# Scoring batch 0 head by head: one operation per head in place of one per query tile, with the order of operations searched anew

## The chip, the core and the metric

The kernel runs on one core of a Trainium2 chip. The metric is the device time of one launch in microseconds; smaller is better. Before the change three runs gave 567.77, 568.21 and 569.11 us, median 568.21 us. The core has a matrix engine (PE, TensorE), a vector engine (DVE), a scalar engine (ACT), a general engine (POOL, GpSimd) and a queue that issues transfers (SP). Each engine works through its own list of instructions in order.

## What is computed

Four batches of eight heads, 576 positions, head size 64. First attention with rotary positions, then a two-layer block with a parametric relu, then a soft mixture of eight experts with four slots each:

```python
q_rot, k_rot = rotate(q), rotate(k)
scores = scale * q_rot @ k_rot.T
attn = exp(scores - max(scores)); attn /= sum(attn) + 1e-09
x = attn @ v                              # 2304 x 512
h = x @ w_in                              # 512 -> 2048
x = (max(h, 0) + alpha * min(h, 0)) @ w_out
logits = x @ phi                          # 32 slots
# softmax over tokens gathers 32 slot inputs, 8 experts relu(s @ w1) @ w2,
# softmax over slots spreads the outputs back over 2304 rows
```

## The kernel before

The attention works on a pair of heads (four pairs per batch) and, in each pair, on four tiles of 128 query rows and a tail of 64. The two heads of a pair lie on the two halves of the 128 partitions: head 0 on partitions 0 to 63, head 1 on 64 to 127. For each tile and head PE computes 128 x 576 scores, as two pieces of 288 columns (j = 0, 1) that fill two banks of PSUM, the tile `st`. DVE takes the row maximum (`top`, L449), ACT the exponential and its sum (`expo`, L454) and adds a small constant (L471), DVE takes the reciprocal (L472), POOL scales the row (`norm`, L496).

In batch 0 PE then transposes the result (`turn`, L519, and `turn_c`, L570), ACT copies it out (L529, L574), and PE multiplies with v (L602). The later batches transpose on DVE and through a round trip to DRAM (`tb`, `sc`, `ET`), and their scores use two half-precise factors (`scores`, L444, one pass each), head by head.

In batch 0 the scores are plain 32-bit matmuls with a contraction of 64 (`plain`, L431). The operation `plain` scores both heads of a tile: for each j it issues head 0 and then head 1, each to its own `st` tile. It takes two `st` slots at once, and only two exist (`st=2` in the plan, 2 buffers of two banks in `ps_s`). So both slots have to be free before a tile is scored. The first tile of all is split by j instead: one operation for the left pieces of both heads, one for the right.

Next to batch 0 run the conversion of the first weight matrix into two half-precise parts (DVE L671 to L675, ACT L683 and L686, PE L248 and L249 `rest`, ACT L242 `dg` and L253), the folding of the second with phi (L724, L733), and the rotary products of the coming pairs on POOL (L331, L339). After batch 0 the first layer starts (L763 `ph`, twelve matmuls for a chunk).

Nothing in the program is scheduled while it runs. A table (`ORDER`) lists all operations of the plan in one order, `plan.order()` decodes it and checks that no operation stands before one that it needs and that no slot is taken before it is free, and the operations are then issued in that order, each to its engine.

Of the kernel before, what the change touches and what calls it, by code (L numbers as in the profile page):

```python
# [11 lines left out]
F32 = mybir.dt.float32  # L12
# [7 lines left out]
B, H, S, D = 4, 8, 576, 64  # L20
# [20 lines left out]
    "NvCW+tpA6dA6h1+XiTMD_B&Z5|7;rGKbW}ocQ+x7?zd^4_FK0jq^TI3Lv{lkl3DauRO_lYfup-m8We~}V?}1&%ko+tcc={cb6~e+)%dI}6AB|I1J71j|>D5(Ty(<wuwyg#0@>AQg-jpr"
    "p)Qw+T{y2Pt(^hEK1Ey~C;w*4$8dzQi;+In_T=KMR^0eT}_d&Nfc0le6*tz@{of+?Sg3We5-uU&-EqgYVs~VxzrNnLbp7JJ}vh%5_-"
    "z1u@U77vZMZP+l(%J}Nprg=HIDlt;L)+1ESOkZU=YgsFOB;*0gU6Srm#?l~s&yg4C4E$(d^n_0qr-"
    "}xQSlVhfAYmCkH}5Ys~)8fj67z1dy~~pt5%a+exl0pCU;>%a>~xTb0Was3_jXdwu3bAmYhtOP~)24Y*w}Ktl>A8hJVsIH|Ow%)1NnJG}G;JNBG0sqN;X`<;via$6q_Pe>51Qy-"
    ";i7?N5`ZXPdV<ms(}~BOd+eWe8cAV$yUj$9a`!V$w~&&AYM{^4t;5`|r+aUK;c61MJNlqWJd-$M^GcH^)+^Qtl{p{#*-JWo{=|M>DFm<k4mO8}G-(Z||r-"
    "cYYgW@BMLZP*$DQMenqd&G9=jn+znIuXH~>7Oq=D<xi8rx=U|!oSefVWdk25E?f#*>N{=U`b$?YP_X+zMTE<dBBkUaNoGgE`Lm;!ioT0^m_7<RWE0zD8+>3Y(|<<b^-"
    "%cA7@+w)mHI7pMU<jgV@sJTzMny{Cv@^((-"
    "kxI@7vG5u);s>PxjgayWr)uTbvB4%^;=RtaTDI0}K}pS#v0N7(8j7^=K@>S(pe<d<zHZCyn_0q5q!5lprQ)Y8_G53gfC*hZKgHoNyZX1a>d#oIzJxlv$9KTGDD*uw>e#^{uW}-"
    "7QSS>~OkX6g*!N@|mIvvwhna|B=<|adXmpx5ZM$UlEWPzK>+r9;HGL8W=|1IOgDc>xR>cIEI>))Ftu%A^IvUDKU}86-"
    "Blyj61bzjQ)VStEp19n~`>kp??cGD*bRcqd8#sn>JZ9#k9#_)cvvK{c(>7Xif<3H<g+Vp{=K-(wdvc;AV=y?&J`^JJ(9@EohM|8aBqwicy_i1tY-HcNKK`Sfq4HoAetc?T0nC?#Ph-"  # L50
    "H9bx=U3$6X$8!`Tc7LUu$`(>DBglC70ouhjgX2Gn{Nnbm9RQKx7N0cN4UY7BF_F4aBdOm|l=YQ$Ns6whYI;*~gHpBeytT)R&|esvnK#aDKEL?FJ8%xon{+=;$t*Lq`~|3n#peTt?tZt-"
    "J4b$es&~|OP()3TC&0Gt+kUnw-U{;Tsr%R1WmP!5mqzWX9J&$GV$Hh`d1r|3m5({bq=)<2NcZ{a?$LOmh&y(;g3{4}yeyr&RL3eZbS!-"
    "TLqgNVnGYjm8~YXLZTn%}(6@<y=2GL}@+wWqJ%HHjRcBU3Z<;lkEcro|62M-4HX``f=C48)MmHYtjf>seyp@vu9kj-0LgKXFoP$=A%ixg?IozP}6%`f~lr(N>-"
    "osRqo$U!P81Q}uUquFudgc7K!&AQ{HYn??@8ctv9h|9bz2>~+eHC7BDX01VH$cjaG4OsiBE>(~>CO0)BMo4AiS@1r#^Ui%;}5|vR}z&?!>Udj%^a%ik{7-"
    "Wcw}xVR!TFxy5YkRrL_GijGz0RPw3o9&BePVM;D!eE}iVbd0vm*60FBS%WGGF)v)ly0ymA!A>omZ0Q1kzl^>KrYZ!TzRmhsdueX@ASJ}k|w1Vv1Nk}rQ?iLTwOLOVaE`8;3cmChCtdFK"
    "g#lJJa)cR5=jNYYF*(y&M>zt>MhZN1*$WFS`6bctj$cd+boO`xKF9E>sPSEV(CU-AfACnfFJS}v-+m*oZX%^9uHN{q?DRATX#-nHM=$74(#lYrq<ufkpN-NC|&5HZa@il+dui3vw^yc;"
    "&h(478(ZKp!$aia>`tF;Qy<0R_Ms3hG{Hb~6P8p*Nyw!CElJr_`{<wqG0F}7Tx+x|l0my*X*K?g7$H<Q^nRPMbq|TXTQ7rYa{rZump$BeX7#J;s851G>^kG)p&-"
    "`#$$L$5BR`J(h%E3gF?g{3;OoUd+v+0+sNNq|Ma&*Zx#q_#Iw_~DLoqQhTdTB+{3?L(>xmJ552PFsUohl<O$4cEJTaFZ@y{3#e*%mw*P-"
# [1535 lines left out]
```

## Time and profile before

| | |
|---|---|
| time, median of three runs | 568.21 us |
| the profiled execution | 567.4 us, its span 565.5 us |
| PE busy | 534.2 us, 94% of the span |
| DVE, ACT, POOL busy | 453.1, 362.7 and 317.0 us |
| busy in the span by stretch | in the rows below |
| chain that ended last, by engine | PE 70%, POOL 8%, ACT 7%, DVE 7%, DMA 5% |

The span is the time from the first to the last instruction; the remaining 1.9 us lie around it. Busy times of PE include the tail of each matmul until its result is written, as the profile models it, so neighbouring matmuls overlap in them. A 32-bit matmul appears as two records, so the four matmuls of a tile of batch 0 appear as eight.

### The profile page before, as it was taken

Reading aid. Unit: us, or ns where it says so; the run is one execution under the profiler, and the core shown is the slowest. Engines: PE = TensorE matmul, PEld = TensorE weight load, DVE = VectorE, ACT = ScalarE, POOL = GpSimd, SP = SyncE. Lnnn points to the kernel's source line nnn. Section 1 sums busy time; section 2 is a strip of 40 time slices with the busy share of each in tenths; the row PEclk is TensorE's granted clock in tenths of the full one; section 3 lists DMA queues with packets and bytes.
Section 4 is the critical chain, followed back from the end, with each engine's and each line's share of the span. In section 5 each row is a group of like instructions: output and inputs, shape, how many; then the busy total and the mean of one; then the engine's idle time right before and its main releaser. Section 6 shows DMA issues by size and latency. Waiting matters only on the chain.

```text
span 565.5 us, 14971 instructions
## 1 busy us (share of the span) xinstructions
PE 534.2 (94%) x5770; PEld 395.0 (70%) x5770; DVE 453.1 (80%) x1049; ACT 362.7 (64%) x951; POOL 317.0 (56%) x299
## 2 busy tenths in 40 slices
PE   3789999999999999999999999999999999999984
PEld 1445545578877787787777688778778888863573
DVE  5699988898998788899898889898864899754541
ACT  2999989998878668878766778687342323330221
POOL 0799978889998668779884778675110000001000
PEclk9999999999999999999999999999999999999996
DMA  8963855435999987897999897879764999899988
GB/s 305 394 250 110 318 197 184 142 114 163 319 324 323 351 258 253 264 343 255 309 299 304 307 279 277 307 239 315 238 237 173 412 404 349 330 369 379 406 321 249
DMA packets 80807, 160.76 MB, mean 284 GB/s; under 512 B 5344, under 2 KB 44640, under 8 KB 80736
## 3 DMA queue, kind: packets, MB, share of 16 engines
q1 hardware_dynamic: 79408, 158.99, 80.5%
q8 instruction: 46, 0.75, 0.5%
q10 hardware_dynamic: 1328, 0.82, 0.5%
q14 instruction: 25, 0.20, 0.1%
HBM read 115.75 MB, written 36.96 MB: 270 GB/s over the span
## 4 chain that ended last, share of the span: by engine, by line
PE 70%; POOL 8%; ACT 7%; DVE 7%; DMA 5%; issue 2%; SPq 1%; ACTq 0%; POOLq 0%; DVEq 0%
PE ph L763 29%; PE pv L602 10%; PE st L444 8%; PE pu L955 3%; DMA sc<-tb 3%; POOL e L496 3%; PE lg L800 3%; PE ph L1286 3%; PE po L1345 2%; POOL xn L331 2%; PE pt L519 2%; DVE mm L449 2%; DMA vt<-in_v_dram 1%; PE pf L1470 1%; ACT e L454 1%
## 5 line engine op out<-in xcount | busy, mean ns | idle before, releaser
L763 PE MATMUL ph<-xt,w 128*128 128x256 f16 x1536 | 183.8, 273 | 0.0
L763 PEld LDWEIGHTS <-w 128*128 128x128 f16 x1728 | 162.1, 98 | 28.7 <-issue 6.2
L496 POOL TENSOR_SCALAR e<-e,mm 128x576 f32<-128x576 f32 x144 | 121.0, 849 | 72.5 <-DVE mm L472 60.7
L454 ACT ACTIVATE e<-st,mm 128x576 f32<-128x576 f32 x144 | 106.0, 736 | 31.5 <-DVE mm L449 25.1
L449 DVE TENSOR_REDUCE mm<-st 128x1 f32<-128x576 f32 x144 | 106.5, 743 | 16.9 <-PE st L444 10.3
L771 ACT ACTIVATE rl<-ph 128x256 f32<-128x256 f32 x144 | 53.3, 379 | 75.7 <-PE ph L763 66.6
L331 POOL TENSOR_TENSOR xn<-xn,tabs 128x576 f32<-128x576 f32 x60 | 91.5, 1538 | 4.5 <-DMA ks<-xn 2.2
L776 DVE SCALAR_TENSOR_TENSOR g<-rl,oma,ph 128x256 f32<-128x256 f32 x144 | 65.9, 465 | 22.4 <-ACT rl L771 21.8
L506 DVE STREAM_TRANSPOSE tb<-e 128x512 f32<-128x512 f32 (+1 forms) x108 | 75.3, 705 | 5.4 <-DMA sc<-tb 3.9
L602 PE MATMUL pv<-ET,vt 128*64 128x256 f32 (+1 forms) x640 | 77.0, 384 | 0.3 <-ACT ET L574 0.3
L444 PE MATMUL st<-ks,qs 128*128 128x288 f32 x384 | 73.9, 316 | 0.7 <-ACT e L454 0.6
L602 PEld LDWEIGHTS pv<-ET,vt 128*64 128x64 f32 (+1 forms) x640 | 42.4, 136 | 26.4 <-issue 5.2
L444 PEld LDWEIGHTS st<-ks,qs 128*128 128x128 f32 x384 | 54.4, 189 | 6.6 <-issue 2.5
L792 DVE STREAM_TRANSPOSE gb<-g 128x512 f32<-128x512 f32 x64 | 44.0, 694 | 0.1
L356 POOL TENSOR_TENSOR qs<-xn,qs 64x576 fp32r<-64x576 f32 x24 | 34.9, 1454 | 12.4 <-ACT qs L349 4.3
L471 ACT ACTIVATE mm<-mm,eps 128x1 f32<-128x1 f32 x144 | 39.6, 289 | 1.5
L431 PE MATMUL st<-ks 64*128 64x288 f32 (+1 forms) x168 | 30.2, 456 | 9.4 <-DVE ks L304 7.5
L975 POOL MEMSET edt<- 128x256 f32 x1 | 0.5, 497 | 66.6 <-DVE lp L944 66.6
L334 POOL TENSOR_TENSOR xn<-xn 128x576 f32<-128x576 f32 x24 | 34.8, 1454 | 0.9
L359 ACT ACTIVATE ks<-xn 64x576 fp32r<-64x576 f32 x48 | 32.7, 680 | 0.8
L431 PEld LDWEIGHTS st<-ks 64*128 64x128 f32 (+1 forms) x168 | 17.2, 191 | 19.0 <-DVE ks L304 8.4
L454 ACT ACTIVATION_READ_ACCUMULATOR e<-st,mm 128x1 f32 x144 | 28.3, 197 | 0.0
(171 smaller groups left out, 783.6 us busy)
## 6 DMA issues: line engine op xcount, KB each, us to landing
sc<-tb SPq DMA_DIRECT2D x48, 576.0 KB, 4.4
ET<-sc SPq DMA_DIRECT2D x24, 1152.0 KB, 7.0
xw<-in_moe_w_dram SPq DMA_DIRECT2D x42, 512.0 KB, 9.0
xn<-in_k_dram SPq DMA_DIRECT2D x15, 576.0 KB, 6.8
xn<-in_q_dram SPq DMA_DIRECT2D x15, 576.0 KB, 6.4
wraw<-in_moe_w_in_dram SPq DMA_DIRECT2D x8, 1024.0 KB, 9.3
wraw<-in_w_out_t_dram SPq DMA_DIRECT2D x8, 1024.0 KB, 6.0
wor<-in_moe_w_out_dram SPq DMA_DIRECT2D x16, 512.0 KB, 9.4
```

The costliest lines, as they stand in the source:

```text
L331: eng.tensor_tensor(e["x"][:, w], e["x"][:, w], tabs[:, w], ALU.mult)
L431: nc.tensor.matmul(st[to, j, at:at + w], x, k[rows, z:z + w], start=True, stop=True)
L444: nc.tensor.matmul(st[:, j, 0:288], r["q"][:, 768 * h + 128 * s:768 * h + 128 * s + 128].bitcast(F32R), r["k"][:, a, h, ks].bitcast(F32R), ...
L449: nc.vector.tensor_reduce(c["mm"][:, h:h + 1], c["st", h][:, :, 0:288], axis=AX.XY, op=ALU.max, negate=True)
L454: nc.scalar.activation(c["e"][:, h].rearrange("p (a n) -> p a n", a=2), c["st", h][:, :, 0:288], AF.Exp, bias=c["mm"][:, h:h + 1], accum_o ...
L496: nc.gpsimd.tensor_scalar(c["e"][:, h], c["e"][:, h], c["mm"][:, 6 + h:7 + h], 1.0, ALU.mult, ALU.mult)
L506: nc.vector.transpose(out=to if tail else to[:, :, 0:8].rearrange("p q (m h) j -> p q m h j", h=2)[:, :, :, h], in_=e.rearrange("p (m q j) ...
L602: nc.tensor.matmul(pv[r], v[k, 4 * h + i if i < 4 else 8 + (h if b else 0)], x, start=(i == 0), stop=(i == 4))
L763: nc.tensor.matmul(ph, wi[j][:, wp, kc, 128 * fo:128 * fo + 128], xt[:, xp, kc, :], start=(n == 0), stop=(n == 3 * KC - 1),)
L771: nc.scalar.activation(c["r"], c["ph"], AF.Relu, scale=-1.0)
L776: nc.vector.scalar_tensor_tensor(blk["g", j][:, fo, :], c["r"], oma[:, f:f + 1], c["ph"], ALU.mult, ALU.add)
L792: nc.vector.transpose(out=blk["gt", j // 2][:, f % 8 - 1:f % 8 + 1, :].rearrange("p c n -> p (c n)"), in_=blk["g", j][:, fo - 1:fo + 1, :] ...
```

## The change

`plain` now scores one head: it takes one `st` slot, allocates one `st` tile, and issues the two pieces j = 0, 1 of its own head. Each tile of batch 0 has two such operations. The first tile has four, one for each head and j. The operation of the tail is as it was. The table `ORDER` is another one for the whole program; the number of instructions on every engine is the same as before. New line numbers are 3 higher up to the scores and 1 lower after them.

```diff
 ORDER = (
-    "c-m!F2S60p7M(k@EGsO#Ql&~$5Cjo^C?cXUDt<Lm6hRSDqp^N9wy3DlSQCr}dx$kEC=x*I4Mo9%3JPLG=}mfFK-is`Kkv;f;QzB_-"
+    "c-"
...
         exps = []
-        s_st2 = [Slot("st") for h in heads]
         for h in heads:
-            s_st = s_st2[h]
-
-            def plain(js=(0, 1)):
+            s_st = Slot("st")
+
+            def plain(h=h, js=(0, 1)):
+                if 0 in js:
+                    c["st", h] = ps_s.tile([128, 2, 512], F32, tag="st", name="st")
+                st = c["st", h]
                 k, q = r["k"][:, 0, 0], r["k"][:, 0, 1]
-                for g in heads if 0 in js else ():
-                    c["st", g] = ps_s.tile([128, 2, 512], F32, tag="st", name="st")
                 for j in js:
-                    for g in range(2):
+                    for g in (0, 1) if tail else (h,):
                         rows = slice(64 * g, 64 * g + 64)
-                        to, st = (rows, c["st", 0]) if tail else (slice(0, 128), c["st", g])
+                        to = rows if tail else slice(0, 128)
...
-            if b:
-                o = order_ops["s"] = op(PE, 1250 if tail else 530, n + h - ATT, scores, ready + [order_ops["s"]], takes=[s_st], uses=[s_st] + s_qk)
-            elif h:
-                o = order_ops["s"]
-            elif early:
+            if early:
                 ends = qk[b, p][3]
-                o = order_ops["s"] = op(PE, 530, n - ATT, lambda plain=plain: plain(js=(0,)), [ends["k", True], ends["q", True], order_ops["s"]], takes=s_st2, uses=s_st2 + s_qk)
-                o = order_ops["s"] = op(PE, 530, n - ATT + 1.5, lambda plain=plain: plain(js=(1,)), [ends["k", False], o], uses=s_st2 + s_qk)
+                o = order_ops["s"] = op(PE, 530, n + h - ATT, lambda plain=plain: plain(js=(0,)), [ends["k", True], ends["q", True], order_ops["s"]], takes=[s_st], uses=[s_st] + s_qk)
+                o = op(PE, 530, n + h - ATT + 1.5, lambda plain=plain: plain(js=(1,)), [ends["k", False], o], uses=[s_st] + s_qk)
             else:
-                o = order_ops["s"] = op(PE, 1250 if tail else 1070, n - ATT, plain, ready + [order_ops["s"]], takes=s_st2, uses=s_st2 + s_qk)
+                o = order_ops["s"] = op(PE, 1250 if tail else 530, n + h - ATT, scores if b else plain, ready + [order_ops["s"]], takes=[s_st], uses=[s_st] + s_qk)
```

On PE, at the start of the program, the first two tiles stood like this before (`st_138` and `st_139` are the tiles of head 0 and head 1 of the first query tile, `st_170` and `st_171` those of the second):

```order
L431 MATMUL st_138<-ks_134 128x288
L431 MATMUL st_139<-ks_134 128x288
L431 MATMUL st_138<-ks_134 128x288
L431 MATMUL st_139<-ks_134 128x288
L431 MATMUL st_170<-ks_134 128x288
L431 MATMUL st_171<-ks_134 128x288
L431 MATMUL st_170<-ks_134 128x288
L431 MATMUL st_171<-ks_134 128x288
L211 MATMUL top_200<-idf_97,mws_114 128x128
```

and now, in the same place (`st_143` and `st_165` are the first tile, `st_174` and `st_184` the second):

```order
L434 MATMUL st_143<-ks_132 128x288 x2
L434 MATMUL st_165<-ks_132 128x288 x2
L434 MATMUL st_174<-ks_132 128x288 x2
L434 MATMUL st_184<-ks_132 128x288 x2
L518 MATMUL pt_202<-idf_97,e_163 128x128 x4
```

Heads alternated matmul by matmul; now both matmuls of a head stand together.

On PE in the second head pair the scores stood in one piece (`x4` is both heads of a tile; `pv` is the product with v, `rest` a part of the weight conversion):

```order
L602 MATMUL pv<-ET,vt 64x256 x10
L519 MATMUL pt<-idf,e 128x128 x4
L431 MATMUL st<-ks 128x288 x4
L248 MATMUL rest<-w_390,dg 128x512
L249 LDWEIGHTS neg
L249 MATMUL rest<-w_390,neg 128x512
L519 MATMUL pt<-idf,e 128x128 x4
L211 MATMUL top<-idf,mws 128x128
L602 MATMUL pv<-ett,vt 64x64 x10
```

and now some heads stand alone (`x2` is one head), others still beside each other:

```order
L569 MATMUL pc<-idf,e 128x128
L434 MATMUL st<-ks 128x288 x2
L251 MATMUL rest<-wx,dg 128x512
L252 LDWEIGHTS neg
L252 MATMUL rest<-w_177,neg 128x512
L214 MATMUL top<-idf,mws 128x128
L601 MATMUL pv<-ett,vt 64x64 x10
```

Of the 32 heads' operations of batch 0, 13 follow directly on another head's and 19 do not.

On DVE, the start stood like this before (L299 multiplies with the rotary table, L304 adds the halves; the pieces are k left, q left, k right, q right, told apart by their widths 288, 192, 288, 384):

```order
L299 TENSOR_TENSOR xn<-xn,tabs 128x2x288
L299 TENSOR_TENSOR xn<-xn,tabs 128x2x192
L304 TENSOR_TENSOR ks<-xn 128x288
L304 TENSOR_TENSOR ks<-xn 128x192
L299 TENSOR_TENSOR xn<-xn,tabs 128x2x288
L304 TENSOR_TENSOR ks<-xn 128x288
```

and now:

```order
L302 TENSOR_TENSOR xn<-xn,tabs 128x2x288
L307 TENSOR_TENSOR ks<-xn 128x288
L302 TENSOR_TENSOR xn<-xn,tabs 128x2x192
L302 TENSOR_TENSOR xn<-xn,tabs 128x2x288
L307 TENSOR_TENSOR ks<-xn 128x192
L307 TENSOR_TENSOR ks<-xn 128x288
```

The product of the right piece of k now stands ahead of the sum of the left piece of q, which the first scores need.

## Rows read from the trace of the kernel before

**Rows 1.** Busy time of each engine by stretch; columns as its head says.

```profile
core 0: us, PE busy (x) PEld busy (x) DVE busy (x) ACT busy (x) POOL busy (x), PEclk, DMA share, GB/s
0.00:20.00 20.00, 8.63 (x29) 5.21 (x31) 11.84 (x24) 8.94 (x22) 5.61 (x13) 1.00 0.92 332
20.00:118.00 98.00, 90.69 (x626) 52.36 (x622) 86.52 (x164) 91.33 (x230) 86.41 (x61) 1.00 0.62 218
118.00:503.00 385.00, 383.27 (x4423) 306.65 (x4419) 328.30 (x775) 250.03 (x676) 223.12 (x224) 1.00 0.84 289
```

**Rows 2.** Chain that ended last, 20 to 118 us: share of it by line.

```profile
by line: POOL e L496 12.3%; PE pt L519 6.7%; PE st L431 6.6%; issue 5.5%; ACT e L454 5.3%; ACT w L686 5.1%; PE rest L248 4.5%; PE pv L602 4.4%; ACT w L683 4.2%; POOL qs L356 3.9%; DVE w L673 3.4%; DVE w L675 3.4%; ACT ET L529 3.1%; ACT w L2
```

**Rows 3.** PE in order of time: start us, length us, what, records.

```profile
12.04 3.01 PE L431 MATMUL st<-ks 64*128 64x288 f32 x8 [1.83 <-ACT e L454]
...
32.49 1.24 PE L431 MATMUL st<-ks 64*128 64x288 f32 x8
33.66 0.33 PE L570 MATMUL pc<-idf,e 128*128 128x128 f32 x1
```

**Rows 4.** PE in two cuts of that group, until 32.52 and until 32.86 us.

```profile
32.49 0.51 PE L431 MATMUL st<-ks 64*128 64x288 f32 x2
...
32.49 0.76 PE L431 MATMUL st<-ks 64*128 64x288 f32 x4
```

**Rows 5.** Chain in order of time: start us, us, what, records.

```profile
23.89 1.22 PE st L431 x8
...
45.98 1.47 PE st L431 x7
...
52.50 1.50 PE st L431 x7
...
54.08 1.10 PE rest L248 x2
55.17 0.22 PE rest L249
55.39 0.44 PE pt L519 x4
...
56.09 0.95 PE pv L602 x20
...
58.76 1.16 PE st L431 x8
...
119.64 0.53 PE st L444 x4
...
159.83 2.31 PE pv L602 x20
```

**Rows 6.** Groups of PE and DVE, 20 to 118 us: busy, mean ns, idle before.

```profile
L431 PE MATMUL st<-ks 64*128 64x288 f32 (+1 forms) x150 | 23.9, 421 | 0.0
...
L449 DVE TENSOR_REDUCE mm<-st 128x1 f32<-128x576 f32 x32 | 23.5, 743 | 5.5 <-PE st L431 4.7 <-POOL e L496 0.7
```

**Rows 7.** Weight loads of the scores, 20 to 118 us: ns min/median/max; and at 32.49 us.

```profile
L431 PEld LDWEIGHTS st<-ks x146: 129/186/334, 19.9 to 114.0; 64*128 64x128 f32 x106, 64*64 64x64 f32 x40
...
32.49 0.54 PEld L431 LDWEIGHTS st<-ks 64*128 64x128 f32 x6 [0.17 <-issue]
```

**Rows 8.** DVE and ACT at the start, in order of time.

```profile
7.58 0.76 DVE L299 TENSOR_TENSOR xn<-xn,tabs 128x576 f32<-128x576 f32 x1 [0.42 <-DMA xn<-in_k_dram]
8.37 0.46 DVE L304 TENSOR_TENSOR ks<-xn 128x288 f32<-128x288 f32 x1
...
11.16 0.74 ACT L454 ACTIVATE e<-st,mm 128x576 f32<-128x576 f32 x1 [8.45 <-DVE mm L449]
...
11.89 0.73 ACT L454 ACTIVATE e<-st,mm 128x576 f32<-128x576 f32 x1
...
14.12 0.74 ACT L275 ACTIVATE junk<-vt 128x640 f16<-128x640 f32 x1 [1.02 <-DMA vt<-in_v_dram]
```

**Rows 9.** Wait of POOL, 20 to 118 us: in total, times, longest.

```profile
POOL e L496 <- DVE mm L472: 10.0, 7, 1.9
```

More of the change, by code (lines that the diff above doesn't have):

```diff
@@ L41 @@
[L41 to L58, printed above, removed]
@@ new lines @@
+    "L`FT2?tUaWakIq<3LQ?)0&id;0%tUlEZstR0ufE#f*W3u)^J$$hqUXua+PMJf${C>lhPR;rNL*cZ$*Xa=@m;c<f{&r5arM1PIj>Q%2oP~5p<0dFZtX(NMbOV9C;egA=Tp9<ZmL?@1EZH"
+    ")9lg9U*Kd|r)^{O|2=l<?B-}{-"
+    "xi9hm{S<dz5nK`3!C%&;*{_jUNJq~wBibw<)cWKpas3?ID!vb&?F03p)H}1k}zI1iMp<bP<POM6Xiuuo=V)#R)&CZ_SR6H)t*K)I!jcNJ%y*a%e+Z|r;E`GFqTLnsSYxl%$@F|r~?;-"
+    "^cM;yS;)b~Nks^kf4QTS8POenq#OK$dp?cOlK@@MdU0N`9?>xeQI3Yp!$#C@f#x%F)v$9pG(!9)-^oczA+tlgHw5V)UX1-HCGnQWHlhcd&r!`m9W!lDj^-"
+    "xWArU0$_qjSYJ5vVK$D!b5<Je=^W^hn&EumB__1dVJ{5eUhwQH$d>O*K36b)~9!myM!YC<s8d)<Z>-"
@@ new lines @@
+    ")6Zcd*H3VF6m^*3R_cx;IZ|qnVzagU&j89>OpN<Q2wS7WsorF?wpR_Z;hu`^Qmo?MEJDG>We4n~}SOUe_5xwWk-"
+    "(KClEGWqhrEY;2X+rdgv;tRc^t|B>W~zEq76eu3&GMYCVQXg=qS)Ur)w6Tv%`axlI+uS2zT=yY0O!4xRwbk7topM879R+-ii5C|oAZR+F}W(=Yc`N$aOK#oPx-yda?LlO&y_XG=cm>l^"
+    "R~8s^3~nJ_R~WZM+X>A7hl&&?R-3Xr9^J4**g>xf*$WZ8TRz$yiwEYX1>Yj>wM?4@u4k$g|$u$#z&`_+|6zu9Jy#-31}8o-"
+    "}kl~$sPviICS3I^u5b37cSqsJZAdTv!@D|r1Z=zSO*(6Zdq1%;oMml<1Jc40Y)eM%RIeXogd2D$hp02zigTDQj<bZ)IBV6p8ev8_tT9EunRi{Fb9@y)u6=#z8U&xFWft%P701Sxpo+0?"
+    "wvWX7$V^j445_bYs;FiAv6}+9=i(zGJPNb_=gEwub)gldFj%?We}VIqr$f;R}AaD^n&_MRM_~W=ZeSc(Y2{bqxW_llE}9Dx(dhi$nNf8C*1$7r+@m2=mj}>N+&z6M0gQg(v&>6-"
@@ new lines @@
+    "}xy$SHzgI@7CMV91QW?K=DR^?mF+=s{IY8H~i!8$N?jgBTZ&if~2ffliI?puq+2glk@3wNYg&h|6oiycl*z|VS_qT>_JG|>h)!NF~kW4OBvCXk`W0)d-"
+    "kOEe3zxiMtBzw82E?gcrqX6L1@M_4&`u>JWnDC%>SVSN|C|nK+-"
+    "wfJ^{;A&2dIM{y`MW3NfHyQ==$>uv=skD9`G~<!JHAhw9^?4QiH+L~pY7rNpEDxYZatWQ(TMT;m#hTydiZop#rntXu~Aq(fb!GaP5=%tZ}|EbqbdH}s(otB<*{$JAA8lgKGQdSh~YFil"
+    "UYB26F`$*6n0zrYYfz8_RR0{$k6M%Uk#1!HbB7ah%UL_?D%V{Ml-Eq>aMwm7W~<8HNYzLOoMHufMCLTlg9g_Pr{L_jcuyhGz3Mt7lI>ues^kpOzR1ONy3ib>%P1FEZcqWum(l%O<$+`g"
+    "GpeT|CDcetV$if|JxDgQwMPtY}CaDFpas0=lrmB#I;~xBNs(O?aYUL`17W1;FrrG0I{YA*KWBn@%+VD^PszxBSR-"
@@ new lines @@
+    "bcpqPw1WuNNGoTDR!1KdBI`%Dm4{g#Qs1UNJKIcG<3_e<e+PKLWsf~n>178F0Sb;kMJZa^a<n_$U_9n-"
+    "*RkVE%kjJ@jCKknp4MtGFIRQ!?^45ui!nXs(4Y32OhIgFZ?SQKztP^?HxBhA)WqjRqI5i8jA8nz+3O<V41Y2hN+5+Ok5%)*v>FIE2(aA6<emmra%H0A^HU_8}ji<)&^7xuJz0e8hnK|S"
+    "3py+vZh7bp%<HhM0*{0}ws5fEr9j`RbzWv|_0oq1~zb}S6E04~BiX$(2wd1A(!liAE;OMY>8Zem9s<`cnu4CGloR|gC8{lR4GKaZGI5i7%j-"
+    "GSxG5OqynZw{<*X2$7TL~~IIloKZD!=qjHtV(Ut@Xt2rfaq}m_6Y<!=u-272iSxtcZ;&!N{U^+8HINT75B@601!PLZgyEZFFf|*cU5*xPJUgtJ$u3WeM92c#a3Q6^lPVVLiA-zli`!)7"
@@ new lines @@
+    "QAEA?EZR!JX>5(2i(W{=Q#9fwdN8sM6I5QTJa4GMvLTg{IGEAsP)Jq`As};?X-"
+    "V%g;l(qE(`lMnkW4fj4aRU<9S)<x^7qM7JL$@Bx*SEhS^|*)sfHLx5jm`pf=DzOjaH1!YN#_NtO=%8RI;KI%U~@-"
+    "UPB5eGiJ5Aq=>ahjMeD&2TUFbf6<NAN==t4!D^W19Y(a#$_Z*&M#~Zm(Ln+u5jpatOH+&G?g5rSF%^oIj8=McL=5^piy%_>B#JCmi+}`NMAAy!F;%ftifL$SPS%vTXhCz=3#BU1n3!dB"
+    "ozO}Jp?rx8BgJIo%&9xgiP*6;xQ3#LRJ1Z#=@VvoN|mGe(`Te*kOU&VDx|Jh-ic{GqJjn{$e3rP6)(M3QsPpka&9s+5}A04S22VrMnpi$NGP*fxry{AhY?)}8(q!GjhC~-"
+    "GBhm@qc)H~L>iLOQK6}eE)oKbM3bNiGKgj>UPSH;mf|4E1~F7G6_ofBEh1)Ebl{~XODl>(lnA%fix9m2L(^>$I=L8<;pHi#i%TSwHPY%P0s)m8iv-"
@@ L81 @@
+    "N*rzDnw(>0>xFun3v`cX0ALnav|%>b2BZcGak0w{KYm*NqfWQ2LWUXnAE2Ve?EBGI%ErA$^p0!zr$nr~4Dp3D`V$eT?tl46Po5(}v?y4@Iw8?2NWDG)6csQ|{h&>}-"
+    "ZQev#Dg+vZ`IRSx@GZN$TNZk2FS1g%gN(o_kh=EjkL?=C^FB;3$(!EHugrpIa3nSwSa;rcZ{QAKs9SjHpISwGXb-eC$z>vYDANxGvECTVAynKdW$e2cgG_0jc==W$^4Kn1&VCETU{&3`"
+    "hBu~iZAuk|l=t>O*9&{(G7Q15e5llBDu}*{aXB4L8SE>&vzm`n%bZL32lU4fToL+-lhR}zlBVD%q2TS~qTZ`!Wv8KC{-"
+    "s&7%@?aR||2X6S3ZToR#R(KQpG%pR^Ak5G+ai707dJ=6m}z;u#VrZ{S3LbmNYDQtU1>gYG&8~a^Ky%N|4+vM=U|O>i2nhvYecj")
 class Slot:
```

41 lines of the change are left out of this document (17 added, 24 removed).

## The prediction

> **What bounds the kernel now.** I read the busy times by stretch first [rows 1]. From 118 to 503 us PE is busy 383.27 of 385.00 us. So whatever delays the start of that stretch is carried to the end whole; it can't be caught up there. From 20 to 118 us, the rest of batch 0, four engines are nearly full at once: ACT 91.33, PE 90.69, DVE 86.52, POOL 86.41 of 98 us. None of them bounds this stretch alone. The chain of waits says the same [rows 2]: it changes engine all the time, and its largest pieces are POOL's scaling of the rows with 12.3%, PE's transposes with 6.7% and PE's scores of batch 0 with 6.6%. The scores are thus 6.6% of 98 us = 6.5 us of the path there. In the first 20 us PE is busy 8.63 us, and others set the pace.
>
> **What the scores cost before.** In a quiet place a tile, both heads, holds PE from 32.49 to 33.66 us, 1.17 us for eight records [rows 3]. Two cuts through it show how [rows 4]: until 32.52 two records have started, until 32.86 four. The records start in pairs, one of each head, and a pair runs in the time of one. The price of a record alone follows from the transposes, which are 32-bit too: four of 128 columns take 0.44 us [rows 5], 0.11 each, so 288 columns take 0.2475 us. Four pairs are 0.99 us, and 0.18 us is left for the change to the next kind of work. Eight records one after the other would be 1.98 us. So the two heads, on the two halves of the rows of the array, run side by side. This is what the change gives up.
>
> **The change, part by part.** *Scores head by head.* A head has four records, all on the same half of the array, one after the other: 0.99 us. Where the next head follows directly, its first record can run beside the last one of the head ahead. Of the 32 operations 13 follow another: 32 x 4 - 13 = 115 steps of 0.2475 us are 28.5 us, and 19 changes of work at 0.18 us are 3.4 us, together 31.9 us. Before it was 16 x 1.17 = 18.7 us. PE gets 13.2 us more work. The trace shows no 32-bit head alone, so I bound it. From below, a head costs half a tile, 0.58 us, if one half-array were served twice as fast alone: nothing added (the scores of the later batches take 0.53 us for a head, but in one pass [rows 5]). From above, by the matmuls of the weight conversion, two records of 512 columns take 1.10 us [rows 5], so four of 288 take 1.24 us, and 32 of those are 39.7 us, 21 more than before. I take 13.2 us, since the transposes are nearest in form and the pairs at 32.49 fit them.
>
> *How much of it is on the path.* From 20 to 118 us stand 150 score records [rows 6]; four tails have ten each, so 110 / 8 = 13.75 tiles, and 13.75 / 16 of 13.2 us is 11.3 us. All scores of that stretch hold PE 13.75 x 1.17 + 4 x 1.16 (a tail, [rows 5]) = 20.7 us, of which 6.5 us are on the chain, 31%. With the same share, 31% of 11.3 us = 3.5 us come onto the path. Nothing would, if PE's idle time (98 - 90.69 = 7.3 us, more if the modelled tails are counted as free) took it all up; all 11.3 us would, if PE became the bound of the stretch.
>
> *The wait for two free slots.* It goes, and it was cheap. The matmuls of the scores found PE idle for 0.0 us in the stretch [rows 6]; once, at 12.04 us, PE sat 1.83 us until an exponential freed the slots [rows 3]. What is late next there is ACT, which has other work. I take 0 us, at best a gain of 1.8 us. DVE waited 4.7 us for scores [rows 6]: the first head's maximum can start 0.18 us sooner than before, the second's starts about 0.8 us later.
>
> *A rule weighed.* The weight loads of the scores take at least 0.129 us, yet six of the eight have begun by 32.86 us, when only four matmuls have started [rows 4, 7], so loads run beside matmuls, also on their own half. The Trainium skill, "TensorE: Matmul & The Clock Gate", Part 3, says a weight load overlaps a running matmul only when the row groups differ, though Part 2 adds loads into a background buffer. By the strict rule each head alone would show three loads, 32 x 3 x 0.129 = 12.4 us more on PE, and 31% of 86% of that, 3.3 us, would bring the forecast to about 575. The trace speaks for the milder form; as a rival of its own the strict one gets 0.05, which is part of the 0.42 below, since its time lies in that case.
>
> *The order at the start.* The sum of the left piece of q, which the first scores need, now stands behind the product of the right piece of k, which ended at 8.34 us [rows 8]. With 0.4 us for the sum, the first matmul starts at about 8.75 us. PE is slow at that time: the group at 12.04, after 1.83 us of idleness, took 3.01 us against 1.24 us later, both at a granted clock of 1.00, the higher level of 2.4 GHz [rows 1, 3]. At 0.5 us a record the first head is done at 10.8 us and its exponential starts at about 11.5 us, against 11.16; the second, 1.5 us behind, at about 13.0, against 11.89. But then ACT waited until 14.12 us for v [rows 8], and the second exponential, with its sum read out, ends before that. I take 0 us, at most 1 us lost. PE is denser there, so the slow spell could also end sooner; one group at full pace is worth 3.01 - 1.24 = 1.8 us.
>
> *The order elsewhere.* The instructions of every engine are the same in number. In the order of PE the same work stands ahead of the first chunk of the first layer, up to two transposes more and one spread less, so that point moves with batch 0. After it PE is full in either order, and I take 0 us, with 2 us either way for waits that come or go.
>
> The sum: 567.4 (565.5 of span and 1.9 around it) + 3.5 = 570.9 us for the profiled execution. The median shown lies 0.8 us above the profiled time, so I predict 571.7 us.
>
> **Rivals.** *PE's spare time hides it.* For it speaks that PE had 7.3 us of idle time in the stretch and that ACT is fuller; a search for an order may have put the scores where PE is free. Against it, the added 11.3 us is more than those 7.3 us, and in-order engines seldom meet a gap exactly. Time: 568.2, within 1.1 us.
>
> *The new order packs batch 0 better: faster.* POOL waited 10.0 us in seven pieces for the reciprocals of rows [rows 9], and the scaling is the largest piece of the chain. A head that can be scored as soon as one slot is free reaches POOL earlier, and each head no longer waits for its neighbour's bank pair. If a third to a half of the 10.0 us went, and PE's work stayed hidden, the end would come 3.3 to 5 us earlier: 563 to 565 us. The gain is capped by ACT's idle time, 98 - 91.33 = 6.7 us. Against it: PE had no idle time in front of the scores, so the slots weren't what POOL waited for.
>
> *PE becomes the bound of the stretch.* Then all 11.3 us count, and with the start some 12 us: 580 us. It decides where PE's work, 90.69 + 11.3 us, reaches the 98 us, and that it does if the modelled tails are real occupancy; but tails of neighbours overlap, so I hold it unlikely in full. Half of it, 574 to 577, is more likely.
>
> **How the numbers follow.** Within 0.2%, about 1.1 us, a measurement of this kernel can't tell a change. Forecast (1.1 to 7 us slower) 0.42; more than 7 us slower 0.11; hidden 0.18; faster 0.29. So slower 0.53, same 0.18, faster 0.29. If it is slower, I expect 569.5 to 576. With cases of both signs the range that holds 8 in 10 reaches from 563.5, half the waits of POOL gone, to 578, most of PE's added work on the path.
>
> **What would show it.** Right: the score records of a head follow each other by about 0.25 us, PE's scores of batch 0 hold it some 13 us longer in all, and the first chunk of the first layer starts 2 to 6 us later, while the stretch behind it is as long as before. Wrong: a head alone in about 0.6 us, then nothing was given up; or the first chunk at the same time or earlier, then the new order made room; or the first chunk as forecast but another end, then the new order did something behind batch 0 that I did not price.

## The result and the profile after

Four runs of the changed kernel gave 570.70 to 578.38 us, median 575.18 us, against 568.04 us (567.77 to 569.11) for the kernel before. The ratio is 1.0104 with an interval of [1.0064, 1.0144], about 6 us slower; the two medians lie 7.1 us apart. The forecast was 571.7 us, 3.5 us slower. Some executions fall into a slower state, and all ratios here leave those out. The profiled execution took 575.8 us, its span 574.0 us.

First the busy times by stretch, after (the columns are those of rows 1; the third stretch ends with the start of the last chunk there too):

```profile
0.00:20.00 20.00, 8.69 (x27) 6.08 (x28) 11.46 (x22) 8.87 (x21) 6.42 (x12) 1.00 0.90 324
20.00:118.00 98.00, 93.92 (x597) 54.00 (x595) 86.07 (x164) 87.88 (x221) 84.97 (x61) 1.00 0.62 215
118.00:503.00 385.00, 380.43 (x4392) 304.81 (x4391) 330.14 (x772) 249.51 (x676) 226.80 (x226) 1.00 0.83 286
```

From 20 to 118 us PE rose from 90.69 to 93.92 us, while ACT fell from 91.33 to 87.88 and POOL from 86.41 to 84.97 [rows 1]. One engine now stands out, where four were level before. (Batch 0 ends later after, so this stretch, cut at 118 us in both, holds a little less of its work.) The chain of the same stretch, by line, says it more sharply:

```profile
by line: PE st L434 20.8%; PE rest L251 12.9%; PE pv L601 12.7%; PE pt L518 11.6%; ACT e L457 4.1%; DVE wx L672 3.6%; PE wpp L723 3.1%; DVE mm L452 3.0%; PE top L214 2.9%; PE rest L252 2.4%; DVE w L674 2.3%; issue 2.0%; DVE wx L670 1.9%; DV
```

Before, POOL's scaling led with 12.3% and the scores had 6.6% [rows 2]. Now PE's four kinds of work hold 58%, the scores alone 20.8%, and POOL is not among the lines shown.

Next the scores themselves: PE in order of time in the changed kernel (start us, length us, what, records). The first two lines are heads alone, the third two neighbouring heads:

```profile
39.68 1.23 PE L434 MATMUL st<-ks 64*128 64x288 f32 x4
...
41.43 1.23 PE L434 MATMUL st<-ks 64*128 64x288 f32 x4
...
56.65 1.25 PE L434 MATMUL st<-ks 64*128 64x288 f32 x8
```

Eight records of two neighbouring heads take 1.25 us, about as the interleaved tile did, 1.24 us [rows 3]. A head alone takes 1.23 us for four records, so it pays the whole price of a tile. Eight heads stand alone in the new order, one of them next to a tail. The scores' group in the stretch from 20 to 118 us, in the columns of rows 6, and DVE's maxima that wait for it:

```profile
L434 PE MATMUL st<-ks 64*128 64x288 f32 (+3 forms) x149 | 29.6, 437 | 0.1
...
L452 DVE TENSOR_REDUCE mm<-st 128x1 f32<-128x576 f32 x32 | 23.6, 746 | 9.0 <-PE st L434 8.7
```

The scores hold PE 29.6 us in place of 23.9, and DVE waits 8.7 us for them in place of 4.7 [rows 6].

Three points of the program show where the end went. For the first layer (`ph`), `min/median/max` ns of a record and first and last start: before, and after.

```profile
L763 PE MATMUL ph<-xt,w x1536: 269/273/288, 122.3 to 471.6; 128*128 128x256 f16 x192
L763 PE MATMUL ph<-xtail,w x192: 272/273/283, 471.7 to 499.7; 128*128 128x256 f16 x192
```

```profile
L762 PE MATMUL ph<-xt,w x1536: 269/273/288, 125.6 to 477.4; 128*128 128x256 f16 x192
L762 PE MATMUL ph<-xtail,w x192: 272/273/283, 477.5 to 505.5; 128*128 128x256 f16 x192
```

The first chunk starts 3.3 us later. From the first chunk to the start of the last record of this layer it was 377.4 us and is 379.9, 2.5 more. From there to the end of the span it was 65.8 us and is 68.5, 2.7 more. Together 8.5 us, which is 574.0 - 565.5. These are single executions; the experiments below tell which parts come back.

### The profile page after: what moved, and what is told of

The parts are those of the page before. It is cut to its first block, busy times and chain, and to the rows that moved or that the text cites. A ratio compares the mean times of both kernels' runs of the same rounds, so it can differ in the third digit from the quotient of the medians.

```text
span 574.0 us, 14942 instructions
## 1 busy us (share of the span) xinstructions
PE 541.2 (94%) x5770; PEld 399.3 (70%) x5770; DVE 456.0 (79%) x1049; ACT 361.8 (63%) x951; POOL 320.0 (56%) x299
## 4 chain that ended last, share of the span: by engine, by line
PE 77%; DMA 9%; DVE 7%; ACT 2%; SPq 1%; issue 1%; POOL 1%; DVEq 0%; ACTq 0%; POOLq 0%
PE ph L762 30%; PE pv L601 13%; PE st L447 8%; DMA xw<-in_moe_w_dram 4%; PE st L434 4%; PE pu L954 4%; PE lg L799 3%; DMA sc<-tb 3%; PE pt L518 3%; PE rest L251 2%; DMA xn<-in_k_dram 2%; DVE mm L452 1%; PE ph L1285 1%; PE st L443 1%; PE pf L1469 1%
## 5 line engine op out<-in xcount | busy, mean ns | idle before, releaser
L495 POOL TENSOR_SCALAR e<-e,mm 128x576 f32<-128x576 f32 x144 | 124.4, 872 | 74.9 <-DVE mm L471 67.8
L434 PE MATMUL st<-ks 64*128 64x288 f32 (+1 forms) x168 | 36.3, 469 | 10.6 <-DVE ks L307 10.5
L434 PEld LDWEIGHTS st<-ks 64*128 64x128 f32 (+1 forms) x168 | 21.5, 199 | 20.9 <-DVE ks L307 8.8
L611 ACT ACTIVATE xt<-pv,vb 128x256 f16<-128x256 f32 x32 | 14.9, 469 | 21.6 <-PE pv L601 21.5
```

The costliest lines, as they stand in the source:

```text
L434: nc.tensor.matmul(st[to, j, at:at + w], x, k[rows, z:z + w], start=True, stop=True)
L495: nc.gpsimd.tensor_scalar(c["e"][:, h], c["e"][:, h], c["mm"][:, 6 + h:7 + h], 1.0, ALU.mult, ALU.mult)
```

## The experiments

The theory to test: PE's work in batch 0 got longer through the heads that stand alone, and this lies on the path. The rivals: the code change itself costs (heads no longer interleaved matmul by matmul); the cost comes from the start of the program; or it comes from the new order behind batch 0.

### The new code in the old order

The second head's operation stands right behind the first's, in the table of the kernel before:

```diff
+        for x in table(ORDER_OLD, [x for x in self.ops if not (x.mark and x.mark[2])]):
+            old.append(x)
+            if x.mark:
+                old.append(second[x.mark[0], x.mark[1], 1, x.mark[3]])
```

> The changed code (one operation per head) in the order of the kernel before: each head's operation stands where the tile's stood, the second right behind the first, nothing else moved. Step of the prediction: heads one behind the other run one after the other but for one record, so a tile holds PE 1.7 to 1.9 us and the kernel is 2 to 6 us slower than before (570 to 574). Rival, from the trace after, where eight records of two neighbouring heads took 1.25 us: neighbours run side by side whatever their order, a tile takes 1.2 us, and the time is that of before within 1 us (567 to 569).

568.55 us, ratio 0.9985 [0.9967, 1.0003]. The code change costs nothing that can be told, nor does it gain. The two heads of a tile, now two operations behind each other, took 1.25 us for eight records, and the first chunk started at 122.5 us. My step "a head behind another, one after the other" is refuted, and the whole slowdown belongs to the order of operations.

### The old order with the second heads moved apart

The same kernel, but the second head and what hangs on it move behind the next short piece of work on PE, where that keeps to the slots; 30 heads then stand alone.

```diff
+            for j in range(i + 1, len(order)):
+                z = order[j]
+                if any(d in late for d in z.deps):
+                    late.add(z)
+                elif z.eng == "PE" and z.cost < 2000:
+                    break
+            trial = order[:i] + [z for z in order[i + 1:j + 1] if z not in late] + [z for z in order[i:j + 1] if z in late] + order[j + 1:]
```

> As split_old_order, but the second head of 15 tiles stands one piece of PE work later, so that nearly every head is alone on PE. Theory that heads alone are what costs: PE gets 30 x 0.61 = 18 us more in batch 0 than before, the first chunk of the first layer comes 6 to 14 us later than in the kernel before (122.5 us), and the time is 574 to 582. Rival (the new order elsewhere is what costs, PE has room in batch 0): within 2 us of split_old_order.

584.04 us, ratio 1.0269 [1.0242, 1.0297]. The first layer and the chain from 20 to 138 us there:

```profile
L876 PE MATMUL ph<-xt,w x1536: 269/273/288, 139.8 to 488.3; 128*128 128x256 f16 x192
```

```profile
by line: PE st L544 30.3%; PE rest L361 13.7%; PE pv L715 12.6%; PE pt L632 10.6%; issue 4.0%; POOL e L609 3.1%; PE wpp L837 3.0%; PE rest L362 2.9%; PE top L324 2.9%; PE pc L683 2.5%; ACT e L567 1.9%; DVE w L784 1.7%; PE wphp L846 1.6%; DV
```

The first chunk is 17.3 us later than the 122.5 us of the run above, more than the 6 to 14 us that I expected, and the time lies above my 574 to 582. Added up group by group, these 30 heads take 41.2 us on PE, the same 15 tiles in the run above 22.5 us, so PE got 18.7 us more. Nearly all of it reached the path, not 31%. A part of the 17.3 us is not the heads' own: the slow spell at the start, told below, lasted until about 30 us here.

### The two orders spliced at the first chunk

The new order up to the first chunk and the old one behind it, and the other way round:

```diff
+        n = next(i for i, x in enumerate(new) if x.ph)
+        first = set(new[:n])
+        return new[:n] + [x for x in old if x not in first]
```

> The new order up to the first chunk of the first layer, the rest in the order of before. If batch 0 in the new order is what costs: 571 to 576, nearly the changed kernel. If the new order behind batch 0 costs as much as the profiled runs suggest (3.1 us of 8.5 up to the first chunk, the rest behind it): 570 to 572, and the stretch from the first chunk to the end as long as before (443 us).

> The order of before (heads of a tile side by side) up to the first chunk of the first layer, the rest in the new order. If batch 0 is what costs: 567 to 569, the time of before. If the new order behind it costs: 572 to 575, and more spread between runs than before has.

575.88 us, ratio 1.0104 [1.0073, 1.0134], and 574.09 us, ratio 1.0097 [1.0074, 1.0119]. Each half of the new order costs about as much as the whole did, so the two don't add up and the medians alone don't place the loss. The profiles help further. In the first splice the rest behind the first chunk took 443.0 us, as before (443.2). In the second, whose batch 0 has the old order and no head alone, the first chunk came at 125.3 us all the same: it was 1.8 us late already at 34 us, behind a longer slow spell, and at the seam PE waited 0.8 us for ACT. Its end, behind the last chunk, was 2.1 us longer than before. It did not spread more than the kernel before (3.4 against 3.7 us), as I had thought it might. In the profiled execution of the first splice, the granted clock fell in batch 0, which the profile after doesn't show there (stretches in the columns of rows 1, then PE in order of time):

```profile
36.00:42.00 6.00, 4.27 (x28) 2.31 (x27) 5.96 (x14) 4.34 (x9) 4.89 (x5) 1.00 0.37 111
42.00:46.00 4.00, 3.95 (x11) 2.19 (x11) 3.93 (x10) 3.12 (x9) 2.31 (x3) 0.57 0.44 169
46.00:50.00 4.00, 4.00 (x11) 2.06 (x9) 4.00 (x6) 2.38 (x7) 3.92 (x3) 0.58 0.00 0
50.00:54.00 4.00, 4.00 (x16) 2.03 (x16) 2.18 (x4) 3.40 (x9) 2.67 (x2) 1.00 0.00 0
```

```profile
40.47 0.49 PE L289 MATMUL top<-idf,mws 128*128 128x128 f32 x2 [1.73 <-ACT w L761]
40.89 1.23 PE L509 MATMUL st<-ks 64*128 64x288 f32 x4
...
42.83 2.29 PE L509 MATMUL st<-ks 64*128 64x288 f32 x4
```

From 42 to 50 us the clock was at 0.57, most of the time at the lower level of 1.2 GHz; a head alone took 2.29 us there in place of 1.23. PE had waited 1.73 us for ACT shortly before. The first chunk came at 131.3 us, 5.7 us later than with the same order in the profile after. The two of its six runs with the highest mean clock (0.993 and 0.994) took 572.5 and 572.1 us, the four at 0.986 to 0.989 took 575.7 to 577.5. By those two, the new batch 0 in front of the old rest costs about 3 us (572.3 against 569.28); this picks two runs by their clock, and no profile fell on them.

### Two trials that told little

In ten tiles of the new order the two heads were put next to each other: the second pulled up where the slots allow it, otherwise the first pushed back with all that hangs on it. And the new order was left for the old one at the place nearest to the last chunk where the old one fits on.

```diff
+            up = up[:i + 1] + [y] + up[i + 1:]
+            down = later(order, x, y)
...
+            order = up if self.fits(up) else down if self.fits(down) else order
```

```diff
+        n = min(good, key=lambda n: abs(n - m))
+        first = set(a[:n])
+        return a[:n] + [x for x in b if x not in first]
```

> The changed kernel with its order, but the first head of each tile moved back to stand right ahead of the second (with what depends on it), so that no head of batch 0 is alone on PE; ten tiles are touched. Theory that heads alone cost: eight heads of 1.23 us become half of a 1.25 us pair, 4.9 us less PE work, the first chunk comes 2 to 5 us earlier than in the changed kernel (125.6 us), time 570 to 573. Rival (the new order's other moves cost, or the moved heads come too late): 574 or more.

> The changed kernel with its order up to the last chunk of the first layer, and the order of before behind it. The profiles have 68.5 us behind the last chunk in the changed kernel, 67.9 in old_then_new, and 65.6 to 65.8 in the four with the old tail. If the new tail costs what these say: 2 to 3 us faster than the changed kernel, 572 to 573, and 65.7 us behind the last chunk. If the tail only follows the transfers that start at the end of attention: the same time as the changed kernel, 575.

597.97 us, ratio 1.0508 [1.0461, 1.0556], and 581.18 us, ratio 1.0243 [1.0207, 1.0279]. In the first, moving the heads and their successors cost far more than joining could give: its first chunk came at 149.4 us, with PE idle for longer and its granted clock down to 0.83 in places (40 to 50 us, 90 to 110 us). In the second the first chunk came at 124.9 us, but the splice itself held up the weights of the experts: PE waited 7.4 us for them at once, and 75.7 us lay behind the last chunk. Neither speaks for or against a theory.

### Idle matmuls at the start

Both kernels with sixteen matmuls of the identity ahead of everything, to see whether the slow first groups of PE explain the later first chunk. The first two groups of the kernel after took 2.66 and 2.65 us for eight records, against 1.25 us later.

```diff
+    spare = ps_m.tile([128, 128], F32, tag="pm", name="warm")
+    for _ in range(16):
+        nc.tensor.matmul(spare, idf, idf, start=True, stop=True)
```

> The kernel before, with 16 matmuls of the identity (result unused) on PE while it waits for the first transfers, up to about 7 us. If the half pace of PE in the first 20 us comes from its idleness and lies on the path: the group at 12.04 us takes 1.25 in place of 3.01 us, and the time falls by 1 to 2 us. If the first 20 us are bound by transfers and ACT: groups faster, time unchanged within 1 us.

> The changed kernel with the same 16 matmuls. There PE kept half pace until about 28 us; its groups at 17.88 and 23.34 and the weight parts at 26.48 took some 5 us more than at full pace, and the chain runs through them. If that is part of the loss: 2 to 5 us faster than the changed kernel, 570 to 573. If not: 574 to 576.

569.50 us, ratio 1.0023 [1.0000, 1.0046], and 571.90 us, ratio 1.0075 [1.0038, 1.0113], on a chip where the kernel after was not run beside them. The kernel before gained nothing (first chunk at 122.4 us), though its group at 12.04 us fell from 3.01 us [rows 3] to 1.96: others set the pace there. In the kernel after the first chunk moved to 123.5 us, with the groups behind the first one 1.4 us ahead, but of the same lengths (PE in order of time, then two stretches in the columns of rows 1):

```profile
8.52 1.61 PE L434 MATMUL st<-ks 64*128 64x288 f32 x8 [1.83 <-DVE ks L307]
11.82 2.65 PE L434 MATMUL st<-ks 64*128 64x288 f32 x8 [1.70 <-DVE ks L307]
...
16.52 3.63 PE L434 MATMUL st<-ks 64*128 64x288 f32 x8
...
21.98 2.30 PE L434 MATMUL st<-ks 64*128 64x288 f32 x8
```

```profile
8.00:20.00 12.00, 9.00 (x29) 5.89 (x29) 9.19 (x17) 8.45 (x23) 6.04 (x6) 0.64 1.04 399
20.00:28.00 8.00, 6.51 (x22) 3.70 (x22) 5.59 (x14) 6.31 (x17) 5.36 (x4) 0.69 1.05 389
```

So an earlier start takes 1.6 to 2.1 us off the delay of the new order, and the idle matmuls did not take these groups out of the slow spell. They did make its clock visible: 0.64 and 0.69 granted. The profile after reads 1.00 for groups of the same lengths, but that is no reading. Its trace has no clock record ahead of 28.5 us, where one at full speed begins, and the column shows 1.00 where there is none. In the kernel before the first record begins at 20.7 us. With the idle matmuls in the kernel after the records begin early and show the lower level from 11.3 to 25.0 us.

### Heads alone made dearer and cheaper

The kernel after again, and twice with only the eight heads alone changed: their matmuls issued twice, or scored in one pass on the upper 16 bits of both factors.

```diff
-                        for z, w, at in pieces:
+                        for z, w, at in pieces * (2 if ("alone", h) in c else 1):
```

```diff
-                            nc.tensor.matmul(st[to, j, at:at + w], x, k[rows, z:z + w], start=True, stop=True)
+                            kk = k[rows, z:z + w]
+                            nc.tensor.matmul(st[to, j, at:at + w], short(x) if one else x, short(kk) if one else kk, start=True, stop=True)
```

> The kernel after once more, as the mark for the two others of this chip. Both theories: 1.010 times the kernel before, about 574 to 575 us, first chunk of the first layer at about 125.6 us.

> The kernel after, but the eight heads that stand alone in PE's order issue their two matmuls twice, the second time over the first. A head alone took 1.23 us, so PE gets 8 x 1.0 to 1.23 = 8 to 10 us more in batch 0 and nothing else changes. Theory (PE sets the pace of batch 0, all of its added time lies on the path): first chunk at 133.5 to 135.5 us, the time 8 to 10 us above after. Rival (the 31% of my prediction): 2.5 to 3 us above after. Rival (ACT or POOL sets the pace, the delay of the first chunk came from the start of the program): within 1 us of after.

> The kernel after, but the eight heads that stand alone in PE's order are scored in one pass, on the upper 16 bits of both factors alone (the lower 16 bits are left out). A head of four records becomes one of two; at about 0.12 us each in place of 0.25 to 0.31 that is 0.3 to 0.5 us in place of 1.23, so PE does 6 to 7.5 us less in batch 0, more than the 4.9 us that being alone costs. Theory (all of PE's time is on the path): first chunk at 118 to 120 us, the time 6 to 7.5 us below after, at or below the kernel before. Rival (31%): about 2 us below after. Rival (the delay comes from the start and other engines): first chunk as in after, 125 to 126 us. If other engines take over once PE has less to do, the gain ends near the 3.3 us by which the first chunk is late: 570.5 to 571.5 us.

After again: 577.03 us, ratio 1.0140 [1.0095, 1.0185]. Doubled: 579.7 us by the runs that the ratio uses, ratio 1.0206 [1.0149, 1.0263]. One pass: 573.16 us, ratio 1.0086 [1.0047, 1.0125]. Both intervals overlap that of after again, so the times alone decide little: doubled lies 2.7 us above after again by the medians and 3.8 us by the ratios, not 8 to 10, and nearer to the 31% rival. What follows rests on the first chunk of one profile each. A head alone and the first layer, in the doubled kernel and in the one of one pass:

```profile
39.40 2.20 PE L438 MATMUL st<-ks 64*128 64x288 f32 x8
```

```profile
L768 PE MATMUL ph<-xt,w x1536: 268/273/288, 131.7 to 479.4; 128*128 128x256 f16 x192
```

```profile
37.92 0.42 PE L442 MATMUL st<-ks 64*128 64x288 bf16 x2
```

```profile
L772 PE MATMUL ph<-xt,w x1536: 270/273/288, 122.4 to 470.8; 128*128 128x256 f16 x192
```

In the kernel after again the first chunk started at 125.1 us. Doubling gave PE 8 x (2.20 - 1.23) = 7.8 us and moved the chunk by 6.6 us; I had expected 8 to 10 us, since I took each repeat for 1.0 to 1.23 us and it took 0.97. One pass took 8 x (1.23 - 0.42) = 6.5 us from PE and moved it by 2.7 us, to 122.4 us, where the kernel before had it.

A part of these moves happened ahead of the first head alone, where the three kernels do the same. The first tile of the second pair shows it; it stands between the start and all eight heads alone. After, after again, one pass, doubled, after with idle matmuls:

```profile
33.86 1.37 PE L434 MATMUL st<-ks 64*128 64x288 f32 x8
```

```profile
33.42 1.37 PE L434 MATMUL st<-ks 64*128 64x288 f32 x8
```

```profile
32.65 1.37 PE L442 MATMUL st<-ks 64*128 64x288 f32 x8
```

```profile
33.58 1.37 PE L438 MATMUL st<-ks 64*128 64x288 f32 x8
```

```profile
31.86 1.37 PE L434 MATMUL st<-ks 64*128 64x288 f32 x8
```

| kernel | this tile starts | first chunk starts | between |
|---|---|---|---|
| before | 32.49 | 122.3 | 89.8 us |
| new code in the old order | 32.71 | 122.5 | 89.8 us |
| after | 33.86 | 125.6 | 91.7 us |
| after again | 33.42 | 125.1 | 91.7 us |
| after with idle matmuls | 31.86 | 123.5 | 91.6 us |
| one pass | 32.65 | 122.4 | 89.8 us |
| doubled | 33.58 | 131.7 | 98.1 us |

This parts the 3.3 us of the later first chunk. Behind the tile the new order costs 1.9 us, the same in each execution, and one pass gives these 1.9 us back whole; doubling adds 6.4 us, 82% of its 7.8. Ahead of the tile the new order was 0.9 to 1.4 us late, 0.2 us in the execution of one pass, and 0.6 us early with idle matmuls. This is the slow spell: its end, by the first clock record at full speed, came at 28.5 us after, at 28.0 again, at 26.4 with one pass and at 25.0 with idle matmuls. The old order had it at about 21 us in three executions, but at 26.0 in the second splice, which was 1.8 us late there with the old order. So it is not shown that the new order makes the spell longer.

Past those 1.9 us taking work from PE gave nothing: 6.5 us less brought no more than the new order had cost. Other engines take over there, as the chain from 20 to 122 us of the kernel of one pass shows:

```profile
by line: POOL e L505 11.9%; POOL xn L339 10.8%; PE st L442 7.8%; issue 6.7%; PE pv L611 6.5%; PE pt L528 5.8%; ACT e L465 5.4%; PE rest L256 5.3%; DVE mm L460 5.1%; ACT w L695 3.2%; POOL xn L342 3.0%; ACT ET L538 3.0%; ACT w L261 2.5%; ACT 
```

POOL's scaling leads again with 11.9%, next to the 12.3% of the kernel before [rows 2]. So from that tile to the first chunk batch 0 has a floor of about 89.8 us. That the engines beside PE set it is read from the chain; no run tried it. The heads alone add 8 x (1.23 - 0.62) = 4.9 us to PE; some 3 us of it are hidden under that floor, and 1.9 us come through. The median is 3.9 us below after again; at 573.16 us it still lies above the 570.5 to 571.5 us that I expected if other engines take over. With the first chunk of before, this kernel still stays 4.9 us behind before by the medians, and 2.6 us by the profiled spans (568.1 against 565.5). That loss lies further back.

### The stage of the experts, across all runs

No run was made for this alone; the profiles of the runs above tell it. The expert stage of PE runs from the end of `px` to the last of `po` (the second product of the experts). Both rows, first of before, then of after:

```profile
L1230 PE MATMUL px<-wo,xtail x64: 379/379/403, 509.3 to 512.6; 128*32 128x256 f32 x64
L1345 PE MATMUL po<-xw,hz x384: 272/273/404, 530.4 to 553.3; 128*32 128x128 f32 x130, 128*32 128x256 f32 x62
```

```profile
L1229 PE MATMUL px<-wo,xtail x64: 379/379/403, 515.2 to 518.5; 128*32 128x256 f32 x64
L1344 PE MATMUL po<-xw,hz x384: 272/273/404, 536.6 to 562.4; 128*32 128x128 f32 x128, 128*32 128x256 f32 x64
```

Between the last starts lie 40.7 us before and 43.9 us after. Over the runs with either rest of the order:

| rest of the order | runs | last `px` to last `po` | last chunk to the end |
|---|---|---|---|
| old | before, new code in the old order, heads moved apart, new then old, before with idle matmuls | 40.5 to 40.7 us | 65.5 to 65.8 us |
| new | after, after again, one pass, doubled, old then new, after with idle matmuls | 43.3 to 45.3 us | 67.9 to 70.0 us |

The two sets don't overlap, and it makes no difference which order stood in batch 0. The trial with joined heads fits the new set (44.9 and 69.4 us); the one that left for the old order behind the last chunk fits neither, for its wait of 7.4 us. The new order costs 2 to 4 us here; the upper end is from executions whose granted clock fell in this stage (0.96 over it in after again). Where it held (after, doubled, old then new) the stage took 43.3 to 43.9 us, 2.6 to 3.4 us more. PE's waits in this stage, after (engine, line, releaser: us, times, longest):

```profile
PE pf L1469 <- DVE ob L1474: 1.2, 2, 0.8
PE ph L1285 <- DMA xw<-in_moe_w_dram: 1.1, 1, 1.1
PE pf L1469 <- DVE mov L1374: 0.6, 1, 0.6
PE pst L1239 <- DVE phs L1255: 0.3, 1, 0.3
PE pe L1433 <- DVE wph L1314: 0.2, 1, 0.2
```

They sum to 3.4 us; before they were 1.8 us, with no wait for expert weights among them. That is half of the 3.2 us. The other half is PE's own busy time, 1.6 us more in that stretch, with nearly the same instructions. The new order cuts `po` into ten pieces between other work, where it stood in six, which may be the reason. Busy times by stretch, before and then after:

```profile
512.90:553.60 40.70, 38.82 (x591) 23.60 (x587) 19.84 (x68) 8.01 (x17) 1.90 (x2) 1.00 0.97 368
```

```profile
518.80:562.80 44.00, 40.44 (x590) 23.10 (x586) 19.15 (x69) 8.73 (x18) 0.24 (x1) 1.00 0.94 349
```

Neither half was tried by an experiment that worked, so it is shown that the order of this stage costs, but not by which of its moves.

The first layer's stretch shows no such split: 376.4 to 380.0 us with the new rest, 376.7 to 379.2 us with the old. The 2.5 us more in the profile after is of that execution, since the same kernel took 377.1 us there when it ran again; one wait of PE for the load of the round trip (`pv` for `ET`) was 1.8 us of it, and 0.7 us the second time.

## Why the prediction was right in direction and short in size

The time fell inside the range, and added work on PE in batch 0 did reach the path. In the working one price was right; the number of dear heads, the start and the order elsewhere were wrong. That the first chunk came near its forecast is luck.

*Scores head by head: the price of a head right, the count wrong.* I let neighbouring heads run one after another but for one record and charged 13.2 us. They run side by side, 1.25 us for eight records; only heads alone cost, and there are eight, not 32. The price I gave a head alone was right: 0.99 us and 0.18 for the change of work, 1.17, and one holds PE from 39.68 us to the next piece of work at 40.84, 1.16 us:

```profile
39.68 1.23 PE L434 MATMUL st<-ks 64*128 64x288 f32 x4
40.84 0.66 PE L518 MATMUL pt<-idf,e 128*128 128x128 f32 x4
```

Against half a tile, 0.58 us, that is 0.58 us more for each, 4.6 us for eight (4.9 by the lengths of the groups). The scores' group rose by 5.7 us in the stretch, not by 11.3, and some of that is groups still in the slow spell.

*The share on the path: near by luck.* I took 31%, the share of the scores on the chain of before. Measured, 1.9 of some 4.9 us came through, 39%. But a share of a chain tells where the path ran, not what added work does: of the next 7.8 us 82% came through, and with 30 heads alone nearly all. Batch 0 behaves as the later of two times, a floor by the other engines and PE. For the first chunk 3.5 us were forecast, all from the heads; 3.3 and 2.8 us were measured, 1.9 from the heads and the rest from the start, which I had put at nothing.

*The wait for two free slots: right.* Nothing was gained: in the stretch DVE's maxima wait longer for scores than before.

*The start: wrong by about 1 us.* I let it cost nothing. The first matmul of the scores came at 8.85 us, close to the 8.75 I worked out, but the groups behind ran at the slow pace for longer. I had also taken the 1.00 in the clock column for a reading; the trace has no clock record there.

```profile
13.20 2.65 PE L434 MATMUL st<-ks 64*128 64x288 f32 x8 [1.69 <-DVE ks L307]
...
17.88 3.63 PE L434 MATMUL st<-ks 64*128 64x288 f32 x8
...
23.34 2.30 PE L434 MATMUL st<-ks 64*128 64x288 f32 x8
```

In the stretch behind 20 us of before a group took 1.22 us [rows 5]; here one at 23.34 us still took 2.30. By the first tile of the second pair this cost 1.4 us, and 0.9 us when the kernel ran again. Whether the order or the execution makes it so is open.

*The order elsewhere: wrong in size.* I wrote 0 with 2 us either way for the order behind batch 0. The stage of the experts lost 2.1 to 4.2 us, as much as batch 0. I had compared the order of PE only up to the first chunk, and trusted that PE being full in the layer's stretch covered what follows; but in the last 66 us PE waits for DVE and, in the new order, for the experts' weights, which rows 1 don't show, as they end at 503 us. This is the third of my signs of being wrong: the first chunk as forecast, but another end.

*The rule weighed.* Its time, 575 us, was met, but not by its mechanism: the weight loads of a head alone did not make it dearer than a tile, nor than the 1.17 us that I had worked out without them. The Trainium skill, "TensorE: Matmul & The Clock Gate", Part 3, also says there that matmuls start and end strictly in program order. The trace disagrees for heads behind each other: both matmuls of one head stand ahead of those of the other in the program, yet a cut through the group at 56.65 us, 0.25 us in, shows two records begun, where the same cut through a head alone shows one:

```profile
56.65 0.52 PE L434 MATMUL st<-ks 64*128 64x288 f32 x2
...
39.68 0.51 PE L434 MATMUL st<-ks 64*128 64x288 f32 x1
```

*The rivals.* "Hidden" and "faster" did not come: the floor of the other engines hid about 3 of the 4.9 us, not all, and no run with the new batch 0 had its first chunk earlier than 122.3 us. "PE becomes the bound" names the mechanism of batch 0 in part: PE is the later time there, but by 1.9 us only.

## What to carry to other kernels

Where several engines are level, price added work as the later of two times, the engine's own and the floor of the others; not as its share of the chain. Here two half-height matmul groups that stand next to each other share the array, whether interleaved or not; moved apart, each pays the full price, so keep such pairs adjacent when an order is searched. Before a difference between two executions is put down to an edit, look at a point ahead of the edit: here up to 1.2 us was there already, between executions that do the same up to that point. When a table reorders a whole program, compare the stages behind the edited one too, each by its own start and end.

## What the runs showed of the hardware

Eight records on one half of the array took 2.20 us, but four on one half followed by four on the other 1.25 us. So records of the second half started ahead of records of the first that were still waiting, as the cut at 56.65 us shows.

PE's first groups ran at about half the later pace, until some 20 us before and 28 us after. The clock column reads 1.00 there only because the trace has no clock record yet. With sixteen matmuls ahead it has them, 0.64 and 0.69, and the kernel after kept the lengths of all groups but the first. At the start of a program the length of a known group is the better witness.

The runs of the kernel after spread over 7.7 us on one chip and 6.0 us on another, those of the kernel before over 1.3 and 5.7 us, and with the new order the longer ones mostly go with a lower mean of the granted clock: after again, 573.2 us at 0.995, 578.3 to 579.2 us at 0.984 to 0.986. The first splice's profile shows one such dip, at 42 to 50 us, and the trial with joined heads has 0.83 from 40 to 50 us. Whether the long runs of the kernel after have it at the same place stays open, since no profile fell on one.
